# A linear-attention and MLP block on one core: the first row block of W1 loaded as two halves of its columns

## The chip, the cores and the metric

The kernel runs on one core of a Trainium2 chip. The metric is the device time of one execution in microseconds; for the kernel before it is 205.89 us, the median of three runs.

## The reference

The input x has 2048 tokens of width 640. It is normalized per token, and the result feeds two branches whose outputs are added to x. Cut to what matters:

```python
xn = layernorm(x)                         # 2048 x 640, no scale or offset
# branch A: linear attention, 32 heads of 20
q, k, v = split(xn @ wqkv)                # wqkv is 640 x 1920
phi = lambda t: where(t > 0, t + 1, exp(t)) + 1e-6
o = phi(q) @ (phi(k)^T v) / (phi(q) . sum(phi(k)) + 1e-6)
# branch B: MLP
h = gelu(xn @ w1 + b1)                    # w1 is 640 x 1536
out = x + o @ wo + (h @ w2 + b2)          # w2 is 1536 x 640
```

All tensors are bf16.

## The kernel before, in words

The kernel is written for each engine by hand. A small planner (`Pl.ins`) records every instruction on its engine in the order of the Python text, and puts a semaphore wait ahead of an instruction wherever a resource that it reads or writes was last touched by another engine or a DMA. The resources are names such as `r_W1[k]` (row block k of W1), `r_x[t]` (token tile t of x) and `r_xnT[t]` (the transposed normalized tile t); each DMA has its own semaphore. Nothing reorders the instructions afterwards, so the order in the text is the order on each engine, and an instruction that waits holds up everything behind it on its engine.

Tokens come in 16 tiles of 128. The 640 rows of W1 are five row blocks of 128 (`DT` = 5, index k), and its 1536 columns are twelve column blocks of 128 (`JT` = 12, index jb). The hidden layer is computed first, transposed: for each jb, five matmuls with the stationary block `W1[:, k, jb]` and the moving tile `xnT[:, k, tokens]` add up in PSUM, and ScalarE applies the gelu into `HG`. After that follow the keys (L563, L569), the products of phi(k) with xn (L596, L605), the queries (L648), the small matrices of the attention (L658 to L712), and the output matmuls (L768, L779), which end the kernel.

The change is in the first microseconds, where x and W1 arrive while TensorE has nothing to do yet. SyncE's queue issues the loads in this order; the second part of x tile 0 goes from ScalarE's queue at the same time:

```python
dma_x(1, 1)
dma_w1(0)
dma_w1(1)
dma_w1(2)
dma_x(2, 1)
dma_w1(3)
dma_x(3, 1)
dma_w1(4)
```

`dma_w1(k)` moves one row block of 128 rows with 1536 columns, 3072 bytes a row. Four loads of two x tiles each follow, and then DMA transposes that wait for normalized tiles.

Meanwhile TensorE runs fillers (L321) and six matmuls on constants that open banks 0 to 5 (L453). VectorE computes the statistics of tiles 0 and 1 (`ln_half` L357, `ln_aggr` L365), GpSimd the reciprocal root (L367), and VectorE the normalization (`ln_norm` L381). TensorE transposes tile 0 in three parts and tile 1 in two (`tr_part` L342); ScalarE copies them to `xnT` (`cp_part` L350), except for the second part of tile 1, which is VectorE's (L351).

The first two token tiles are then computed in an order of their own, by `hk` (L439), which does the matmuls of one jb for given row blocks k and tiles, with all twelve column blocks of two tiles held in six PSUM banks. This order lets TensorE begin with row block 0 alone:

- k=0 for tile 0, jb 0 to 11 (12 matmuls of 128 columns);
- "T1": the transposes of tile 1 (5, L342);
- k=1 for tile 0, then k=0 and k=1 for tile 1 (36 matmuls);
- k=2 for both tiles (12 matmuls of 256 columns), then k=3 for jb 0 to 7;
- "T2": the transposes of tile 2 (`transp`, 5, L389);
- k=4 for jb 0 to 7, then k=3 and k=4 for jb 8 to 11.

With the last k of an odd jb the gelus of two column blocks follow on ScalarE (L446). Tiles 2 and 3 come next in packs of four column blocks (`h_pack`, L423), and the others in units of two and four tiles (`h_unit`, L408). `h_pack` and `h_unit` read all of `r_W1`. Later in the kernel W1's memory is used again for other tensors, whose first writers list all of `r_W1` too.

Of the kernel before, what the change touches and what calls it, by code (L numbers as in the profile page):

```python
# [112 lines left out]
def bass_parallel_sum__linear_attn_block__dense_activation_gelu__prompt_kernel(  # L113
    nc: bass.Bass, A_x, A_wqkv, A_wo, B_x, B_w1, B_b1, B_w2, B_b2, out):
    Batch, S, D = A_x.shape
    F = B_w1.shape[1]
# [5 lines left out]
    DT = D // P  # L122
    JT = F // P
# [15 lines left out]
    R_ = Pl.res  # L139

    with contextlib.ExitStack() as es:
# [13 lines left out]
        W1 = W1f[:].rearrange("p (k f) -> p k f", k=DT)  # L155
# [54 lines left out]
        def bank(b, lo=0, hi=512):  # L210
            return ps[:, b * 512 + lo: b * 512 + hi]
# [6 lines left out]
        r_xb = [R_("xb%d" % t) for t in range(NT)]  # L218
        r_xn = [[R_("xn%d_%d" % (t, i)) for i in range(2 if t == 0 else 1)] for t in range(NT)]
        r_xnT = [[R_("xnT%d_%d" % (t, i)) for i in range((3, 2)[t] if t < 2 else 1)] for t in range(NT)]  # L220
        r_W1 = [R_("W1_%d" % k) for k in range(DT)]
        r_Wk = R_("Wk")
        r_Wq, r_Wv, r_W2 = R_("Wq"), R_("Wv"), R_("W2")
        r_Wo = [R_("Wo%d" % w) for w in range(NW)]
# [27 lines left out]
        w1v = B_w1.rearrange("(k p) n -> p k n", p=P)  # L252
# [7 lines left out]
        def dma(eng, dst, src, writes, reads=()):  # L260
            Pl.ins(eng, lambda e: e.dma_start(dst, src), reads=reads, writes=writes, dma=True)  # L261
# [4 lines left out]
        def dma_x(t, n):  # L266
            dma("sync", x_in[:, t:t + n, :], xv[t * P:(t + n) * P, :].rearrange("(t p) d -> p t d", p=P),
                sum(r_x[t:t + n], []))

        def dma_w1(k):  # L270
            dma("sync", W1[:, k, :], w1v[:, k, :], [r_W1[k]])

        XA = 3 * P
        for i, (lo, hi) in enumerate(((0, XA), (XA, D))):
            dma(("sync", s_)[i], x_in[:, 0, lo:hi], xv[0:P, lo:hi], [r_x[0][i]])
        dma_x(1, 1)
        dma_w1(0)
        dma_w1(1)
        dma_w1(2)
        dma_x(2, 1)  # L280
        dma_w1(3)
# [14 lines left out]
               reads=[r_ident], writes=[r_ident])  # L296
# [39 lines left out]
        def xT(t, k):  # L336
            return r_xnT[t][next(i for i, (_, lo, hi, _) in enumerate(PARTS[t]) if lo <= k < hi)]
# [97 lines left out]
        def hk(t, n, jb, ks):  # L435
            b = jb // 2
            o = (jb % 2) * 2 * P + t * P
            tok = slice(t * P, (t + n) * P)
            Pl.ins(pe, [(lambda e, k=k: e.matmul(  # L439
                bank(b, o, o + n * P), W1[:, k, jb * P:(jb + 1) * P], xnT[:, k, tok],  # L440
                start=False, stop=(jb % 2 == 1 and k == DT - 1))) for k in ks],
                reads=[r_W1[k] for k in ks] + [xT(u, k) for u in range(t, t + n) for k in ks],
                writes=[B_[b]])
            if DT - 1 in ks and jb % 2:
                for i in range(2):
                    Pl.ins(s_, lambda e, i=i, jb=jb - 1 + i: e.activation(  # L446
                        HG[:, jb, tok], bank(b, i * n * P, (i + 1) * n * P), ACT.Gelu_apprx_tanh, bias=b1c[:, jb:jb + 1]),
                        reads=[B_[b], r_b1c], writes=[r_HG[u][jb - 1 + i] for u in range(t, t + n)])
# [3 lines left out]
        for b in range(6):  # L452
            Pl.ins(pe, lambda e, b=b: e.matmul(  # L453
                bank(b), nc.const_aps.tensor(1.0, [P, P], BF16), pm[:].broadcast_to((P, 512)), start=True, stop=False),
                reads=[r_pm], writes=[B_[b]])
# [49 lines left out]
        for u in plan:  # L505
            if u == "T1":
                for i in range(2):
                    tr_part(1, i)
                    cp_part(1, i)
                ln_stats(2)  # L510
                ln_half(3, 0)
                ln_half(3, 1)
                ln_norm(2)
                ln_aggr(3)
            elif u == "T2":
                at(7)
                b = transp(2)
                ln_norm(3)
                xnT_dma(3)
                xnT_copy(2, b)  # L520
                ln_stats(4)
                ln_rest()
            elif len(u) == 2:
                h_pack(*u)
            elif len(u) == 4:
                hk(*u)
            else:
                h_unit(*u)
# [29 lines left out]
        for c in range(NC):  # L558
            ts = range(c * CH, c * CH + CH)
            cc = slice(c * CW, (c + 1) * CW)  # L560
            for t in ts:
# [4 lines left out]
                    reads=r_xnT[t] + [r_Wk], writes=[B_[b]])  # L566
# [5 lines left out]
                reads=sum((r_xnT[t] for t in ts), []) + [r_Wk], writes=[B_[b]])  # L572
            phi(bank(b), b, 1, PKT[:, cc], r_PKT[c], [])
            dma_t("sync", PK[:, c * CH:(c + 1) * CH, MW:D], PKT[:, cc], [r_PKr[c]] + sum((r_x[t] for t in ts), []),
                  reads=[r_PKT[c]])
# [12 lines left out]
        for k in range(DT):  # L588
            for i in range(DT):
                Pl.ins(g, lambda e, k=k, i=i: e.tensor_copy(plain(Wqkv[:, k, D:2 * D], i), parts(Wqkv[:, k, 0:D], i)),  # L590
                       reads=[r_Wq], writes=[r_Wk, r_WqP])
# [248 lines left out]
        t = NT - 1  # L840
        xb(t)
        tok = slice(t * P, (t + 1) * P)
        for i, (lo, hi, b) in enumerate([(0, 3 * P, bb[1]), (3 * P, MW, bb[2])]):
# [5 lines left out]
                reads=[B_[b], r_xb[t]], writes=[r_o] + ([r_out[s]] if i == 0 else []))  # L849
# [41 lines left out]
```

## Time and profile before

| | |
|---|---|
| median of 3 runs | 205.89 us (205.84 to 206.03) |
| the profiled execution | 206.18 us, span 204.5 us |
| TensorE busy | 200.7 us, 98% of the span, 1238 matmuls |
| TensorE weight loads busy | 104.6 us, 51% |
| VectorE, ScalarE, GpSimd busy | 108.8, 71.3, 33.5 us |
| DMA queue of SyncE | 17.86 MB, 33.8% of 16 engines' span |
| loads of W1, issue to landing | 4.6 us the shortest, 5.6 the median, 6.1 the longest |

The span is the part of the execution in which engines work; the time of the profiled execution is 1.7 us longer. TensorE is busy for nearly all of it. A busy share is an average over the kernel, so for a change in the first microseconds the timeline and the waits of that stretch count, and not the table. The granted TensorE clock is full in all slices. The five loads of W1's row blocks are issued from 1.73 to 4.99 us, and the DMA engines are busy from about 2 us to 13 us.

### The profile page before, as it was taken

What the parts mean: (1) busy time and instruction counts of PE and PEld (TensorE: products, weight loads), DVE (VectorE), ACT (ScalarE), POOL (GpSimd) and SP (SyncE); (2) the same over time, 40 slices, a digit from 0 to 9 for tenths busy, and PEclk for the clock granted to TensorE, in tenths of its full rate; (3) what the DMA queues carried; (4) which work ended last, traced back from release to release, by engine and by line L of the source; (5) the groups of instructions that cost most, each with busy time, mean ns of one, the idle gap of its engine ahead of it and who ended that gap; (6) DMA issues with size and microseconds to landing.
All of it is one profiled execution on the core that took longest, in us unless ns stands there. A gap on an engine that the chain in (4) does not pass through costs nothing.

```text
span 204.5 us, 3358 instructions
## 1 busy us (share of the span) xinstructions
PE 200.7 (98%) x1238; PEld 104.6 (51%) x1238; DVE 108.8 (53%) x238; ACT 71.3 (35%) x144; POOL 33.5 (16%) x84
## 2 busy tenths in 40 slices
PE   8899999999999999999999999999999999999995
PEld 3899884444444444444546444544444444444443
DVE  3588764000007889399748888834634723513131
ACT  2269995666676555121154464500000000000000
POOL 3245637300000001897000200000000000000000
PEclk9999999999999999999999999999999999999999
DMA  5997595799800111100050001239985511102301
GB/s 170 370 265 93 116 179 101 216 329 353 282 7 0 26 26 26 29 0 0 0 99 2 0 0 21 86 52 201 326 217 131 140 42 52 51 26 51 79 29 51
DMA packets 35769, 21.70 MB, mean 106 GB/s; under 512 B 22696, under 2 KB 35112, under 8 KB 35752
## 3 DMA queue, kind: packets, MB, share of 16 engines
q1 hardware_dynamic: 31696, 17.86, 33.8%
q10 hardware_dynamic: 4056, 3.61, 6.6%
q8 instruction: 10, 0.16, 0.4%
q14 instruction: 7, 0.06, 0.1%
HBM read 13.08 MB, written 2.62 MB: 77 GB/s over the span
## 4 chain that ended last, share of the span: by engine, by line
PE 96%; DMA 2%; SPq 0%; DVE 0%; issue 0%
PE ps L768 29%; PE ps L408 19%; PE ps L648 11%; PE ps L596 8%; PE ps L563 8%; PE ps L779 7%; PE ps L439 3%; PE ps L423 3%; DMA W<-in_B_w_dram 2%; PE ps L605 2%; PE ps L569 2%; PE ps L702 1%; PE ps L658 1%; PE ps L712 1%; SPq L261 0%; DVE W L847 0%
## 5 line engine op out<-in xcount | busy, mean ns | idle before, releaser
L768 PE MATMUL ps<-W,HG 128*128 128x512 bf16 (+2 forms) x204 | 43.9, 367 | 0.0
L408 PE MATMUL ps<-xnT,W 128*128 128x512 bf16 (+1 forms) x225 | 39.1, 336 | 0.0
L768 PEld LDWEIGHTS ps<-W,HG 128*128 128x128 bf16 x204 | 19.5, 98 | 22.2 <-ACT Msb L684 0.2
L551 ACT ACTIVATE ek<-ps 128x512 bf16<-128x512 f32 x40 | 23.8, 597 | 19.6 <-DVE PQ L554 9.3
L408 PEld LDWEIGHTS ps<-xnT,W 128*128 128x128 bf16 x225 | 21.9, 98 | 16.8 <-issue 0.3
L412 ACT ACTIVATE HG<-ps,b1c 128x512 bf16<-128x512 f32 (+1 forms) x45 | 26.3, 670 | 11.3 <-PE ps L408 10.8
L552 DVE TENSOR_SCALAR ek<-ek 128x512 bf16<-128x512 bf16 x40 | 11.4, 286 | 28.3 <-ACT ek L551 28.3
L792 DVE TENSOR_TENSOR W<-ps,xnT 128x512 bf16<-128x512 f32 x15 | 10.4, 691 | 24.9 <-PE ps L768 19.6
L648 PE MATMUL ps<-xnT,Wqkv 128*128 128x512 bf16 x100 | 21.9, 379 | 0.0
L768 PE MATMUL ps<-Msb,PQ 128*128 128x512 bf16 (+2 forms) x85 | 19.6, 366 | 0.0
L563 PE MATMUL ps<-Wqkv,xnT 128*128 128x512 bf16 x80 | 17.9, 379 | 0.0
L596 PE MATMUL ps<-xPK,xn_tm 128*128 128x512 bf16 x80 | 17.4, 379 | 0.0
L590 POOL COPY Wqkv<-Wqkv 128x128 bf16<-128x128 bf16 x25 | 13.5, 540 | 22.4 <-PE ps L569 20.9
L357 DVE BATCH_NORM_STATS2 stats<-xPK 128x6 f32<-128x320 bf16 (+2 forms) x32 | 13.9, 478 | 5.3 <-DMA xPK<-in_A_x_dram 5.3
L648 PEld LDWEIGHTS ps<-xnT,Wqkv 128*128 128x128 bf16 x100 | 9.6, 98 | 11.5
L554 DVE SCALAR_TENSOR_TENSOR PQ<-ps,ek 128x512 bf16<-128x512 f32 x20 | 13.8, 691 | 2.1
L768 PEld LDWEIGHTS ps<-Msb,PQ 128*128 128x128 bf16 x85 | 8.1, 98 | 9.2
L596 PEld LDWEIGHTS ps<-xPK,xn_tm 128*128 128x128 bf16 x80 | 7.8, 98 | 9.4
L563 PEld LDWEIGHTS ps<-Wqkv,xnT 128*128 128x128 bf16 x80 | 7.8, 98 | 9.4
L554 DVE SCALAR_TENSOR_TENSOR xPK<-ps,ek 128x512 bf16<-128x512 f32 x16 | 11.1, 692 | 1.7
L619 DVE TENSOR_TENSOR Msb<-Msb,xPK 128x640 f32<-128x640 f32 x14 | 11.6, 826 | 0.5
L367 POOL TENSOR_TENSOR rstd<-aggr,mhalf 128x1 f32<-128x1 f32 x16 | 10.0, 623 | 7.4 <-DVE aggr L365 7.4
(77 smaller groups left out, 156.6 us busy)
## 6 DMA issues: line engine op xcount, KB each, us to landing
Wqkv<-in_A_wqkv_dram SPq DMA_DIRECT2D x3, 800.0 KB, 6.8
xnT<-in_A_x_dram SPq DMA_DIRECT2D x4, 512.0 KB, 6.5
W<-in_B_w_dram SPq DMA_DIRECT2D x5, 384.0 KB, 5.6
W<-in_B_w_dram SPq DMA_DIRECT2D x1, 1920.0 KB, 13.4
out_dram<-W ACTq DMA_DIRECT2D x15, 128.0 KB, 1.7
xn_tm<-rden ACTq DMA_DIRECT2D x12, 128.0 KB, 3.8
xPK<-in_A_x_dram SPq DMA_DIRECT2D x4, 320.0 KB, 6.9
Wo<-in_A_wo_dram SPq DMA_DIRECT2D x8, 160.0 KB, 8.9
```

The source lines that it names most:

```text
L357: Pl.ins(v, lambda e: e.bn_stats(stats[:, s, 6 * h:6 * h + 6], x_in[:, t, lo:hi]), reads=[r_x[t][min(h, len(r_x[t]) - 1)]], writes=[r_stat ...
L408: Pl.ins(pe, [(lambda e, k=k: e.matmul(bank(b, 0, w), W1[:, k, jb * P:(jb + 1) * P], xnT[:, k, tok], start=(k == 0), stop=(k == DT - 1))) ...
L412: Pl.ins(s_, lambda e: e.activation(HG[:, jb, tok], bank(b, 0, w), ACT.Gelu_apprx_tanh, bias=b1c[:, jb:jb + 1]), reads=[B_[b], r_b1c], wri ...
L551: Pl.ins(s_, lambda e: e.activation(e2, src, ACT.Exp), reads=br, writes=[r_ek[s]])
L554: Pl.ins(v, lambda e: e.scalar_tensor_tensor(out=d2, in0=src, scalar=0.0, in1=e2, op0=ALU.max, op1=ALU.add), reads=br + [r_ek[s]], writes= ...
L563: Pl.ins(pe, [(lambda e, k=k, b=b, t=t: e.matmul(bank(b), xnT[:, k, t * P:(t + 1) * P], Wqkv[:, k, D:D + MW], start=(k == 0), stop=(k == D ...
L590: Pl.ins(g, lambda e, k=k, i=i: e.tensor_copy(plain(Wqkv[:, k, D:2 * D], i), parts(Wqkv[:, k, 0:D], i)), reads=[r_Wq], writes=[r_Wk, r_WqP])
L596: Pl.ins(pe, lambda e, t=t, b=b, f=f, i=i: e.matmul(bank(b), xn_tm[:, t, f * P:(f + 1) * P], PK[:, t, 0:MW], start=(i == 0), stop=(i == NT ...
L619: Pl.ins(v, lambda e, t=t: e.tensor_tensor(out=zsum, in0=zsum, in1=PK[:, t, :], op=ALU.add), reads=[r_PK[t], r_PKr[t // CH], r_zsum], writ ...
L648: Pl.ins(pe, [(lambda e, k=k, j=j, b=b: e.matmul(bank(b), Wqkv[:, k, D + j * P:D + (j + 1) * P], xnT[:, k, cc], start=(k == 0), stop=(k == ...
L768: Pl.ins(pe, [(lambda e, i=i, x=x, bk=bk: e.matmul(bank(bk, 0, x[1] - x[0]), seq[i][0], seq[i][1][:, x[0]:x[1]], start=(i == 0), stop=(i = ...
L779: Pl.ins(pe, lambda e, i=i: e.matmul(bank(b), seq[i][0], seq[i][1], start=(i == 0), stop=(i == NS - 1)), reads=seq[i][2], writes=[B_[b]], ...
```

## The change

Row block 0 of W1 is loaded by two DMAs, columns 0 to 767 and 768 to 1535, issued one after the other from SyncE's queue where the one DMA stood. Each has its own resource and its own semaphore; `r_W1` now has six entries. The matmuls of row block 0 wait for the half that holds their column block: jb 0 to 5 for the first, jb 6 to 11 for the second. The other row blocks are loaded as before.

```diff
-        r_W1 = [R_("W1_%d" % k) for k in range(DT)]
+        r_W1 = [R_("W1_%d" % i) for i in range(DT + 1)]
...
         def dma_w1(k):
-            dma("sync", W1[:, k, :], w1v[:, k, :], [r_W1[k]])
+            dma("sync", W1[:, k, :], w1v[:, k, :], [r_W1[k + 1]])
+
+        def rW(k, jb):
+            return r_W1[k + 1 if k or 2 * jb >= JT else 0]
...
         dma_x(1, 1)
-        dma_w1(0)
+        for i in range(2):
+            half = slice(i * F // 2, (i + 1) * F // 2)
+            dma("sync", W1[:, 0, half], w1v[:, 0, half], [r_W1[i]])
         dma_w1(1)
...
-                reads=[r_W1[k] for k in ks] + [xT(u, k) for u in range(t, t + n) for k in ks],
+                reads=[rW(k, jb) for k in ks] + [xT(u, k) for u in range(t, t + n) for k in ks],
```

On TensorE this adds one wait, at the seventh of the twelve matmuls k=0 of tile 0; on SyncE's queue it adds one issue. The order of all other instructions is unchanged, and their source lines move down by five from `hk` and the functions before it on.

## The prediction

> **What bounds the kernel now.** I read the page first, then the chain of work that ended last, then the timeline of the first 14 us.
>
> ```profile
> PE 200.7 (98%) x1238; PEld 104.6 (51%) x1238; DVE 108.8 (53%) x238; ACT 71.3 (35%) x144; POOL 33.5 (16%) x84
> ...
> PE 96%; DMA 2%; SPq 0%; DVE 0%; issue 0%
> ```
>
> TensorE carries 96% of the chain; DMA has 2%, and the chain in order of time (start, duration, what) shows that all of it is one transfer:
>
> ```profile
> 1.73 4.59 DMA W<-in_B_w_dram
> 6.32 0.05 issue
> 6.37 0.84 PE ps L439 x12
> 7.21 0.28 PE ps L342 x5
> 7.49 4.22 PE ps L439 x56
> 11.71 0.28 PE ps L389 x5
> 11.99 1.75 PE ps L439 x16
> 13.73 6.70 PE ps L423 x120
> 20.43 38.97 PE ps L408 x225
> ```
>
> The first row block of W1, issued at 1.73, lands at 6.32, and the twelve k=0 matmuls start. From there TensorE is listed without a break to 202.17. So only what moves TensorE in the first 14 us, and is not lost again before L423, moves the end; behind L423 a shift passes through one for one.
>
> The chain says nothing of the second block. In the timeline of the weight loads and of ScalarE (start, duration, engine, line):
>
> ```profile
> 5.67 0.28 ACT L350 ACTIVATE xnT<-ps 128x128 bf16<-128x128 bf16 x1 [2.92 <-PE ps L342]
> 5.79 0.23 PEld L342 LDWEIGHTS ps<-ident,xn_tm 128*128 128x128 bf16 x4 [0.23 <-DVE xn_tm L381]
> ...
> 6.36 0.67 PEld L439 LDWEIGHTS ps<-xnT,W 128*128 128x128 bf16 x12 [0.34 <-DMA W<-in_B_w_dram]
> 6.99 0.32 PEld L342 LDWEIGHTS ps<-ident,xn_tm 128*128 128x128 bf16 x5
> 7.34 4.09 PEld L439 LDWEIGHTS ps<-xnT,W 128*128 128x128 bf16 x56
> ```
>
> Five transposes start from 6.994; at the 56 ns from one load to the next that the trace's records have here, the following load would come at 7.273. The first k=1 load starts at 7.336, 63 ns late. The source view of the DMA issue at 2.2 us, W1's second block, gives why:
>
> ```profile
> L261 SPq DMA_DIRECT2D W<-in_B_w_dram x1: 432/432/432, 2.2 to 2.2; - x1
> ...
> DMA to landing us min/median/max: 5.1/5.1/5.1
> ```
>
> 2.198 plus 5.1 is 7.3; the trace's semaphore records put the last of its 16 increments at 7.295, and 7.295 + 0.041 = 7.336. The first block has the same step: last increment 6.321, load 6.363. So TensorE waits twice, for block 0 and, directly behind, for block 1. The second wait is so short that the list of waits does not show it, but it is the **gate**: whatever k=0 does, k=1 starts 0.041 us after block 1 has landed.
>
> Behind it the gates have room. Block 2 is down at 8.243 and first used at 9.36, block 3 at 9.649 and 10.67, block 4 at 11.103 and 11.82. Token tile 2's transposes (L389) load at 11.44; its normalization ends at 11.34, and a load follows such an end by 0.05 (5.35 to 5.40), so the slack is 0.05 us. That chain hangs on the load of x tile 3, landed at 10.086 behind the W1 blocks in the same queue.
>
> **What the Trainium skill says.** "DMA: Bandwidth & Descriptors", section on queues, rings and completion order: one transfer is spread over up to 16 DMA engines, each takes its descriptors in ring order, and only the full 16 increments mean landed. The trace agrees: block 0's increments come from 4.658 to 6.321, fourteen by 5.547, two at 6.160 and 6.321. Its section on latency and other measured facts says two engines of the 16 are usually slower, for a cause it calls uncertain; the trace shows two late increments on every block, but not which engines made them. "Perfetto Trace Analysis", section on the HWDGE DMA instruction: the profiled bar of an issue is not the data movement. Here the bar is 0.43 us and the landing 4.6 to 6.1 us after issue. "DMA: Bandwidth & Descriptors", section on why small descriptors are slow, gives every packet a fixed overhead; the trace agrees, and its own durations price it below.
>
> **The change part by part.**
>
> 1. *Block 0's first half lands earlier.* Same issue time, 1.73, half the bytes. Three things then hold the first k=0 load: the landing, the copy of xnT that ScalarE ends at 5.95 (plus 0.04 to 0.05 for the semaphore), and the four transposes before it in program order, whose last load is at 5.922, next slot 5.978. The earliest start is about 6.00 against 6.363: at most 0.36 us. The landing itself is not in the trace. Bounds: not before x tile 1's last increment at 3.641, not after block 0's own 6.321. On the latest engine half of the 2.68 us between these gives 4.98; if it stalls early and streams late, four packets of 121 ns fewer give 5.84. I take 5.84; either lets TensorE start at about 6.00.
>
> 2. *A second wait, at the seventh k=0 matmul* (jb=6), for the second half. Behind it in TensorE's order are five k=0 matmuls, tile 1's transposes and all of k=1; ScalarE's and VectorE's copies of tile 1 wait for those transposes. Six matmuls at 56 ns from 6.00 end at 6.34; the second half lands at about 6.321 + 0.07 (next item), so the load goes at 6.43 and k=0 issues out by 6.77. Tile 1 is normalized at 6.73, so the transposes go at about 6.78 and are out by 7.06 to 7.1.
>
> 3. *Block 1 lands later, by the split's overhead.* The queue is full: of the answer by stretches (TensorE, weight load, VectorE, ScalarE, GpSimd busy, clock, DMA share, GB/s):
>
> ```profile
> 5.00:6.00 1.00, 0.55 (x8) 0.38 (x7) 0.72 (x4) 0.33 (x2) 0.57 (x2) 1.00 0.99 387
> 6.00:7.00 1.00, 0.83 (x16) 0.66 (x14) 0.45 (x1) 0.68 (x3) 0.17 (x1) 1.00 1.00 335
> ```
>
> The DMA engines are busy 99 to 100%, so extra packet time is delay. Median packets of this queue take 36 ns at 768 B, 55 at 1280 and 121 at 3072: 0.0368 ns per byte and 8 ns fixed. Each engine gets 16 packets of 1536 B in place of 8 of 3072: 8 x 8 = 64 ns more, and one more semaphore write of 9 ns. Sum **0.07 us**. Block 1 lands at 7.37, k=1 loads at 7.41.
>
> 4. *SP issues one transfer more.* Issues here follow each other by 0.47 us, so blocks 1 and 2, x tile 2 and all behind them are issued 0.47 later. Block 1 would be issued at 2.67; the first packets of block 0 ran 1.28 after its issue (1.73 to 3.01), which gives 3.95 for block 1, while the first engine to finish block 0 did so at 4.66. The cover is 0.7 us of backlog on the first engine and over 2 us on the latest, where the gate is; without it the cost is 0.47. SP then has its transposes queued, which wait for VectorE until 12.70 (a 6.2 us wait), so the shift ends there. ScalarE's queue is untouched. I take zero.
>
> 5. *Blocks 2 to 4 and x tiles 2 and 3* shift by the same 0.07, inside slacks of 0.7 to 1.1 for the blocks. Tile 2's transposes shift with the path: 0.07 late both, slack unchanged. Zero. Any later work sees the same bytes; one semaphore more costs nothing that the trace shows.
>
> Sum on the path: item 1 gains up to 0.36 at k=0, of which nothing passes k=1, since the wait for block 1 grows from 0.06 to about 0.35; item 3 costs 0.07. Against the profiled execution (206.18, span 204.5) that is 206.25. This execution lies 0.29 above the median of the runs, 205.89, so the runs should have **205.96**.
>
> **The rivals.**
>
> *The early start counts.* Block 1 comes earlier too, because the first touch of W1 stalls less with smaller packets: of block 0's 128 packets, 26 took over 200 ns, and their excess over 121 ns is 613 ns for each engine on average. If a third went away, block 1 would gain 0.2. TensorE can win at most 7.336 less about 7.07, that is 0.27: 205.62. Against it: nothing in the trace ties the stall to packet size, and 0.27 is under what counts as faster here.
>
> *The stall is paid twice.* Block 1 has no packet over 200 ns, so the stall belongs to the first touch of W1's first rows. If it comes again with the second half, everything behind is later by up to 0.61 + 0.07 = 0.68: 206.57, **slower**. It decides from 0.34 us of repeated stall, some 55%. For it: the second half is a transfer of its own, and the gate is the latest of 16 engines. Against: same rows and neighbouring bytes, and the four later blocks paid at most 57 ns for each engine.
>
> *The issue slot is exposed*: 0.47 late, 206.36. The DMA share of 0.99 speaks against it.
>
> *The first half does not land early*, because the latest engine finishes both halves together. Then k=0 starts at 6.36 as now, and the gate still gives +0.07: the same 205.96.
>
> **How the numbers follow.** About 0.2% (0.41 us) is what a measurement of this kernel can tell from no change. Forecast, with the half that is not early: 0.60. Early start counts: 0.14, of which 0.04 for a bound that I have misread. Stall paid twice or slot exposed: 0.26, of which 0.20 beyond 0.41. So faster 0.04, same 0.76, slower 0.20. The likeliest case alone is 205.85 to 206.10. The range takes in most of the gain and half of the slower case: 205.70 to 206.45.
>
> **What would show it.** In the profile after, the first k=0 load should start near 6.0, with a short wait at the seventh; the first k=1 load should stand 0.04 behind block 1's last increment, near 7.41, after a wait of about 0.3 us on DMA; the chain should name W1's second block as its DMA. I am wrong if block 1 lands before 7.25 or after 7.6, if k=1 starts well behind its landing, or if a new gap opens at tile 2's transposes.

## The result, and the profile after

The kernel became slower: 207.05 us, median of six runs (206.62 to 207.38), against 206.00 for the kernel before in its own six (205.84 to 206.40). The ratio is 1.0046, 95% interval 1.0029 to 1.0063, so about 0.95 us were lost. Ratios are taken over all executions of both kernels and need not be those of the medians, which are 1.05 apart here. One execution of all the runs below, at 208.99 us, ran in a slower state of the chip and is in no ratio. The forecast was 205.96 and the range ended at 206.45. The profiled execution took 207.27, 1.09 more than the one shown of before.

The timeline of the weight loads of the kernel after (start, duration, line, count; lines have moved down by five):

```profile
6.08 0.69 PEld L444 LDWEIGHTS ps<-xnT,W 128*128 128x128 bf16 x12
6.79 0.35 PEld L347 LDWEIGHTS ps<-ident,xn_tm 128*128 128x128 bf16 x5
8.43 4.09 PEld L444 LDWEIGHTS ps<-xnT,W 128*128 128x128 bf16 x56 [1.28 <-DMA W<-in_B_w_dram]
12.53 0.37 PEld L394 LDWEIGHTS ps<-ident,xn_tm 128*128 128x128 bf16 x5
12.86 1.14 PEld L444 LDWEIGHTS ps<-xnT,W 128*128 128x128 bf16 x11
```

In the kernel before, tile 2's transposes (L389 there) started at 11.44:

```profile
11.44 0.38 PEld L389 LDWEIGHTS ps<-ident,xn_tm 128*128 128x128 bf16 x5
```

The split does what it says: k=0 starts at 6.08 in place of 6.36, and tile 1's transposes at 6.79 in place of 6.99. Then TensorE stands still until 8.43. In the list of waits (total, times, longest) a wait that was too short to be listed before is now one of the longest of TensorE:

```profile
PEld ps L444 <- DMA W<-in_B_w_dram: 1.3, 1, 1.3
PE ps L444 <- DMA W<-in_B_w_dram: 1.1, 1, 1.1
```

The chain of waits names the transfer, as the longest pieces in order of time show; its DMA is now W1's block 1, issued at 2.67:

```profile
2.67 5.72 DMA W<-in_B_w_dram
8.43 4.37 PE ps L444 x56
14.83 6.70 PE ps L428 x120
```

L428 starts at 14.83 in place of 13.73 (L423 then), 1.10 later, and the profiled execution is 1.09 longer. All the loss is made before that point.

Block 1's last increment comes at 8.388 in the trace's semaphore records, 7.295 before. Fifteen of its sixteen have come by 7.035, when before fifteen had come by 7.11; the longest packet of the stretch took 1.63 us. The last increment then stays 0.85 to 1.15 us behind the fifteenth on every load from block 2 to block 4. But the others are late too: the median increment (the mean of the eighth and the ninth) of block 1 is at 6.29 after and 5.99 before, that of block 4 at 10.98 and 10.27. x tile 3 lands at 11.19 in place of 10.09, its median increment comes at 9.98 in place of 9.31, and tile 2's transposes load at 12.53 in place of 11.44. So two things stand in this profile: the whole queue is late, by 0.3 to 0.7 us, and one increment of each load comes later still.

### The profile page after: what moved, and what is told of

Its sections match the earlier page's. It is cut to its first block, busy times and chain, and to the rows that moved or that the text cites. A ratio compares the mean times of both kernels' runs of the same rounds, so it can differ in the third digit from the quotient of the medians.

```text
span 205.5 us, 3336 instructions
## 1 busy us (share of the span) xinstructions
PE 199.5 (97%) x1221; PEld 104.7 (51%) x1238; DVE 108.9 (53%) x238; ACT 71.3 (35%) x144; POOL 33.4 (16%) x84
## 4 chain that ended last, share of the span: by engine, by line
PE 71%; DVE 18%; DMA 6%; issue 2%; SPq 1%; ACT 1%; DVEq 0%
PE ps L773 28%; PE ps L413 19%; PE ps L784 7%; PE ps L568 6%; DVE Msb L624 6%; DVE PQ L559 3%; PE ps L428 3%; PE ps L444 3%; DMA W<-in_B_w_dram 3%; PE ps L653 3%; DVE ek L557 2%; DVE xPK L559 2%; DMA Msb<-Msb 2%; DMA xPK<-Msb 1%; PE ps L574 1%
```

## The experiments

At first two theories competed. **P**: packets of half the size cost at the first touch of W1. **Q**: one more transfer in front of block 1 costs, through its place in the queue or the later issue of what follows. Each kernel ran beside the kernel before on its chip; "before" stands at 206.0 to 206.1 in all of them.

**The kernel after once more.**

> The kernel after, unchanged, on the chip of the other runs of this group. Both theories expect +0.6 to +1.3 us against the kernel before, the k=1 loads 0.04 us behind the landing of W1's second block, and that landing between 7.9 and 8.7 us instead of 7.3. If one DMA engine's stall in the first profile was chance, the landing is near 7.4 and the time within 0.2 us of before.

206.83 against 206.07, ratio 1.0041 (1.0026 to 1.0057). Block 1 lands at 8.16, k=1 loads at 8.20. The loss is no chance of one profile. But here too the last increments decide: fourteen of block 1's had come by 6.58 (by 6.61 in the kernel before), the last two at 7.94 and 8.16. Tile 2's transposes waited as well:

```profile
8.20 4.09 PEld L444 LDWEIGHTS ps<-xnT,W 128*128 128x128 bf16 x56 [1.08 <-DMA W<-in_B_w_dram]
12.44 0.28 PEld L394 LDWEIGHTS ps<-ident,xn_tm 128*128 128x128 bf16 x5 [0.15 <-DVE xn_tm L386]
```

**An added transfer with almost no bytes.**

```diff
         dma_w1(0)
+        dma("sync", b2t[:], B_b2[MW:D].rearrange("(p a) -> p a", a=1), [r_b2t])
         dma_w1(1)
...
-        dma("sync", b2t[:], B_b2[MW:D].rearrange("(p a) -> p a", a=1), [r_b2t])
```

> Block 0 stays one transfer; the small load of the last 128 values of b2 (2 bytes a row) moves up from far behind to the place between W1's blocks 0 and 1, so that one more transfer stands ahead of block 1 in SyncE's queue and everything behind it is issued 0.47 us later, with almost no bytes and no 1536-byte packets. Theory Q (a transfer more in the queue, and the later issue, costs): block 1 lands near 8.2, +0.6 to +1.2 us, as in the kernel after. Theory P (packets of half size at the first touch of W1 cost): block 1 lands at 7.3 to 7.45, 0 to +0.15 us.

207.04, ratio 1.0057 (1.0037 to 1.0078). Block 1 lands at 8.27. The loss is there without halves. Here block 0 was late as well, at 7.17, though it was issued at 1.73 as before, so this profile has its wait mostly ahead of k=0, and a later issue doesn't explain that part:

```profile
7.21 0.67 PEld L440 LDWEIGHTS ps<-xnT,W 128*128 128x128 bf16 x12 [0.97 <-DMA W<-in_B_w_dram]
8.31 4.09 PEld L440 LDWEIGHTS ps<-xnT,W 128*128 128x128 bf16 x56 [0.15 <-DMA W<-in_B_w_dram]
```

**Half-size packets without an added transfer.**

```diff
-        dma_w1(0)
+        dma("sync", W1[:, 0, :].rearrange("p (a f) -> p a f", a=2), w1v[:, 0:2, 0:F // 2], [r_W1[0]])
```

> Block 0 stays one transfer with one semaphore, but of 256 packets of 1536 bytes; its second half of columns is filled with block 1's first half, so the output is not the reference's. No issue is added and no other one moves. Theory P: block 1 lands near 8.2, +0.7 to +1.3 us (k=0 also starts later, at 6.4 to 7). Theory Q: block 1 lands 0.07 later, 7.4, and +0.05 to +0.15 us.

206.06 against 206.07, ratio 0.9998 (0.9985 to 1.0010). P is refuted, and with it the packet overhead as anything that can be measured here. The profile is of the longest execution of this kernel (206.89), with block 1 at 7.57.

**Two halves by rows.**

```diff
         for i in range(2):
-            half = slice(i * F // 2, (i + 1) * F // 2)
-            dma("sync", W1[:, 0, half], w1v[:, 0, half], [r_W1[i]])
+            half = slice(i * P // 2, (i + 1) * P // 2)
+            dma("sync", W1[half, 0, :], w1v[half, 0, :], [r_W1[i]])
...  # every k=0 matmul reads r_W1[0] and r_W1[1]
```

> Block 0 as two transfers of 64 rows each, packets of 3072 bytes, 4 for each DMA engine and transfer; every k=0 matmul waits for both. One issue more than before, as many packets and bytes. Theory Q: block 1 lands near 8.2, +0.6 to +1.2 us. Theory P: block 1 at 7.3 to 7.45, 0 to +0.15 us.

206.90, ratio 1.0042 (1.0029 to 1.0055): as slow as the kernel after, with packets of 3072 bytes. Its issues of 64 rows take longer: block 1 was issued at 2.97, 0.77 later than before. But it landed at 6.93, earlier than either theory said. TensorE lost its time elsewhere:

```profile
6.45 0.68 PEld L444 LDWEIGHTS ps<-xnT,W 128*128 128x128 bf16 x12
7.17 0.36 PEld L347 LDWEIGHTS ps<-ident,xn_tm 128*128 128x128 bf16 x5
7.48 4.13 PEld L444 LDWEIGHTS ps<-xnT,W 128*128 128x128 bf16 x56
12.30 0.28 PEld L394 LDWEIGHTS ps<-ident,xn_tm 128*128 128x128 bf16 x5 [0.70 <-DVE xn_tm L386]
```

k=1 was only 0.14 late, but tile 2's transposes waited 0.70 for the normalization, since x tile 3 had landed at 10.99. So there is a **second gate**, and block 1's landing by itself isn't the measure. P was gone; Q had to be divided: **I**, the later issue of block 1 and what follows, and **D**, one transfer more wherever it stands.

**Later issue, nothing added.** The activation's record is moved up so that the DMA can wait for it; ScalarE's order is unchanged.

```diff
         dma_w1(0)
-        dma_w1(1)
+        r_late = R_("late")
+        ...  # ScalarE's first activation also writes r_late
+        dma("sync", W1[:, 1, :], w1v[:, 1, :], [r_W1[1]], [r_late])
...
```

> The kernel before with nothing added to the queue, but the issue of W1's block 1 waits for ScalarE's first activation (which ends at 2.74 us), so block 1 and all behind it are issued at about 2.8 in place of 2.2. Theory I (what costs is that block 1 is issued later, so that the DMA engines come to it before it is ready): block 1 lands at 8.0 to 8.8, +0.7 to +1.4 us. Theory D (what costs is one more transfer in the queue, whenever it is issued): block 1 lands at 7.3 to 7.5, 0 to +0.2 us.

206.55 against 206.02, ratio 1.0027 (1.0017 to 1.0037). Block 1 was issued at 2.78, block 2 at 3.15, which is nearly the kernel after's timing (2.67, 3.15), with no added transfer. It costs 0.53 us: less than I said, far more than D. The profile, of an execution above the median (206.94), has block 1 itself early again (6.81, not the 8.0 to 8.8 of theory I). Block 2 and tile 2's normalization hold TensorE behind k=1 instead:

```profile
7.12 3.25 PEld L440 LDWEIGHTS ps<-xnT,W 128*128 128x128 bf16 x48
10.58 0.77 PEld L440 LDWEIGHTS ps<-xnT,W 128*128 128x128 bf16 x8 [0.21 <-DMA W<-in_B_w_dram]
12.29 0.28 PEld L392 LDWEIGHTS ps<-ident,xn_tm 128*128 128x128 bf16 x5 [0.95 <-DVE xn_tm L384]
```

**The second half from ScalarE's queue**, run twice.

```diff
-            dma("sync", W1[:, 0, half], w1v[:, 0, half], [r_W1[i]])
+            dma(("sync", s_)[i], W1[:, 0, half], w1v[:, 0, half], [r_W1[i]])
```

> The kernel after, with the second half of block 0 issued from ScalarE's queue, ahead of its table load. As many transfers as in the kernel after, but SyncE issues block 1 and all behind it at the times of the kernel before (2.2 us). Theory I: block 1 lands at 7.2 to 7.6, -0.1 to +0.2 us against before. Theory D: block 1 near 8.2, +0.6 to +1.2 us.

> The same kernel as e_half_act once more, for a profile of an execution near its median: 0 to +0.2 us, block 1 at 7.2 to 7.6, if block 1's issue time is what matters.

206.09 (ratio 1.0011, 1.0001 to 1.0021) and 206.37 (1.0019, 1.0005 to 1.0034). Most of the loss is gone although the transfers are as many as in the kernel after. Not all of it: the second interval reaches that of the kernel after, and the times that the ratios count are spread from 205.80 to 208.35. Both profiles fell on executions above the median (206.93 and 206.68), with block 1 at 8.09 and 7.99 and not at theory I's 7.2 to 7.6. In both it is the last increment that is late, 1.38 and 0.98 behind the fifteenth; the median increments, 6.00 and 5.79, are as early as before (5.99). So one late increment of sixteen can cost as much with the issue times of before; the times say that it does so less often.

**The same split at block 3.**

```diff
-        dma_w1(3)
+        for i in range(2):
+            half = slice(i * F // 2, (i + 1) * F // 2)
+            dma("sync", W1[:, 3, half], w1v[:, 3, half], [r_W1[(3, 5)[i]]])
...  # k=3 of jb 6 to 11 reads r_W1[5]
```

> The kernel before with block 3 of W1 loaded as two halves of its columns in place of block 0. As many transfers, packets and bytes as in the kernel after, but the added issue comes at about 4 us, when the DMA engines are behind with earlier transfers. Theory I: blocks 1 and 2 as before, 0 to +0.2 us. Theory D: x tile 3 and block 4 land 0.6 to 1 us later, tile 2's transposes are late, +0.5 to +0.9 us.

206.04 against 206.02, ratio 1.0004 (0.9995 to 1.0012). An added transfer costs nothing here; D is refuted. Blocks 1 and 2 keep their issue times. x tile 3 is issued 0.71 later than before (5.00 and 4.30) and lands at 9.89, not later: at this place the backlog does cover the added issue. The profile is of one of the shortest executions (205.76). It shows where the first gate would let TensorE go: block 1 at 7.00, k=1 with no wait.

```profile
6.14 0.69 PEld L441 LDWEIGHTS ps<-xnT,W 128*128 128x128 bf16 x12 [0.26 <-DMA W<-in_B_w_dram]
6.78 0.32 PEld L344 LDWEIGHTS ps<-ident,xn_tm 128*128 128x128 bf16 x5
7.06 4.13 PEld L441 LDWEIGHTS ps<-xnT,W 128*128 128x128 bf16 x56
```

**More delay, and delay from block 2 on.** Both wait for the third matmul of L453; the first holds back block 1 and all loads behind it, the second block 2 and all behind it. The records of these loads move behind that matmul in the Python text.

```diff
-                reads=[r_pm], writes=[B_[b]])
+                reads=[r_pm], writes=[B_[b]] + ([r_late] if b == 2 else []))
...
-        dma_w1(1)      # the second kernel: dma_w1(2)
+        dma("sync", W1[:, 1, :], w1v[:, 1, :], [r_W1[1]], [r_late])
...
```

> As e_delay, no transfer added, but block 1 and all behind it wait for the third of the six matmuls on constants (L453, ends near 3.4 us), so they are issued 1.2 us later than before. If the cost follows the issue time (theory I), about twice that of e_delay or more: block 1 lands at 8.4 to 9.4, +1.1 to +1.8 us. If a late issue only sets off one stall of a fixed size: +0.4 to +0.9 us.

207.58, ratio 1.0078 (1.0050 to 1.0105). Block 1 was issued at 3.59 and landed at 8.28 in the profile, which is of the shortest execution (206.98):

```profile
8.33 4.09 PEld L430 LDWEIGHTS ps<-xnT,W 128*128 128x128 bf16 x56 [1.18 <-DMA W<-in_B_w_dram]
```

By the medians 1.40 us of delay cost 1.47, where 0.58 cost 0.53: the cost grows with the delay, it is no single stall of fixed size.

> Block 1 is issued at 2.2 us as before; block 2 and all behind it wait for the same matmul and are issued near 3.4, 0.7 us later than before. If the cost arises at block 1, which the engines reach before it is ready: block 1 at 7.3, x tile 3 at 10.0 to 10.3, 0 to +0.2 us. If it is the lateness of the whole queue: x tile 3 lands 0.7 later, near 10.8, and tile 2's transposes hold TensorE, +0.5 to +0.8 us.

206.81, ratio 1.0025 (1.0014 to 1.0036). Block 1, issued at 2.20, landed at 7.28 as before; the profile is of a shorter execution than the median (206.43). Block 2, issued 0.92 later than before, and x tile 3 at 10.53 were late, and the second gate held TensorE:

```profile
7.32 4.09 PEld L431 LDWEIGHTS ps<-xnT,W 128*128 128x128 bf16 x56
11.84 0.28 PEld L381 LDWEIGHTS ps<-ident,xn_tm 128*128 128x128 bf16 x5 [0.43 <-DVE xn_tm L373]
```

So the lateness of all that follows counts, not a stall at block 1 alone.

**The first gate moved.**

```diff
-        plan = ... k_list(0, 1, [1]) + k_list(1, 1, [0]) + k_list(1, 1, [1])
+        plan = ... k_list(1, 1, [0]) + k_list(0, 1, [1]) + k_list(1, 1, [1])
```

> The kernel after, with TensorE's k=0 matmuls of tile 1 moved ahead of the k=1 matmuls of tile 0, so that block 1 is first needed 0.67 us later. If the wait for block 1 is the only gate, TensorE starts them at about 7.7 (after the copies of tile 1) and k=1 near 8.4: +0.3 to +0.5 us against before. If the late queue holds a second gate (x tile 3, then tile 2's transposes, near 12.5 instead of 11.44): +0.7 to +1.1 us, with the wait moved to L394.

206.73, ratio 1.0029 (1.0018 to 1.0041): between the two answers. In its profile block 1 had landed at 6.69 and TensorE waited 0.55 for ScalarE's copy of tile 1, with nothing at L394. It doesn't tell the gates apart; it only shows that the new order has a price of its own.

**Earlier issue**, by moving an x load to ScalarE's queue: tile 1, and then all of tile 0, the latter with the whole block 0 and with the halves.

```diff
-        dma_x(1, 1)
+        dma(s_, x_in[:, 1:2, :], xv[P:2 * P, :].rearrange("(t p) d -> p t d", p=P), r_x[1])
...
-        for i, (lo, hi) in enumerate(((0, XA), (XA, D))):
-            dma(("sync", s_)[i], x_in[:, 0, lo:hi], xv[0:P, lo:hi], [r_x[0][i]])
+        dma(s_, x_in[:, 0, :], xv[0:P, :], r_x[0])
```

> The kernel before, block 0 whole, with the load of x tile 1 issued from ScalarE's queue; as many transfers, W1's blocks and all behind them issued 0.47 us earlier. Theory I: block 1 lands at 6.4 to 7.0, k=1 starts at about 7.1 to 7.3, -0.1 to -0.3 us. Theory D: same number of transfers, no change, -0.1 to +0.1 us.

207.08, ratio 1.0067 (1.0041 to 1.0093): slower, and both answers missed. Block 0 landed at 4.89, but x tile 1, now beside W1 on the other queue, at 5.06 in place of 3.64, and VectorE takes tile 1's statistics ahead of tile 0's normalization. k=0 started at 6.89.

> The kernel before, block 0 whole, with all of x tile 0 in one load from ScalarE's queue; SyncE starts with x tile 1, so W1's blocks and all behind them are issued 0.47 us earlier than before, with one transfer less. If the time follows the issue times in this direction too: block 1 at 6.5 to 7.0, TensorE held by tile 0's later normalization and tile 1's transposes instead, -0.1 to -0.3 us, faster than both kernels. If the queue is limited by bytes once it runs at the issue times of before: -0.1 to +0.1 us. If x tiles 0 and 1 arriving together late hold VectorE: +0.2 to +0.5.

206.80, ratio 1.0054 (1.0034 to 1.0074): 0.73 slower, beyond all three answers. The queue did what theory I says: issued 0.47 earlier, block 1 landed at 6.01, 1.28 earlier than before, and x tile 3 at 8.99. TensorE doesn't wait for a DMA at all; it waits for tile 0, whose single load landed at 3.89 in place of 3.04 and 3.23:

```profile
6.25 0.10 PEld L341 LDWEIGHTS ps<-ident,xn_tm 128*128 128x128 bf16 x1 [1.56 <-DVE xn_tm L380]
...
6.92 0.69 PEld L438 LDWEIGHTS ps<-xnT,W 128*128 128x128 bf16 x12
7.63 0.36 PEld L341 LDWEIGHTS ps<-ident,xn_tm 128*128 128x128 bf16 x5
7.95 4.13 PEld L438 LDWEIGHTS ps<-xnT,W 128*128 128x128 bf16 x56
```

> The kernel after, halves of block 0 and all, with all of x tile 0 from ScalarE's queue; SyncE issues block 1 and all behind it at the times of the kernel before (2.2 us), and all of W1 stays on SyncE's queue. If the lost time of the kernel after is its later issues and nothing else: -0.2 to +0.2 us against before. If the halves cost by themselves: +0.5 to +1.0.

206.68, ratio 1.0031 (1.0020 to 1.0042): the time is tile 0's again (k=0 at 6.84, no DMA wait later), so it can't say what the halves cost. What it does show is the queue: with the issue times of before, halves and all, block 1 lands at 6.79 and x tile 3 at 10.01, not later than before.

No kernel here beats the kernel before.

**The runs side by side.** Issue and landing are read from the trace. "Stalled" is worked out from its packet records: for blocks 0 and 1 of W1, as many packets as they have in order of start, the time of every packet above the median for its size, added up and divided by 16 engines. "Median" is x tile 3's median increment. Each row is one profile.

| kernel | block 1, 2 issued | block 1 lands | x tile 3 lands | median | stalled | ratio |
|---|---|---|---|---|---|---|
| before | 2.20, 2.67 | 7.30 | 10.09 | 9.31 | 0.63 | 1 |
| half-size packets | 2.20, 2.71 | 7.57 | 10.35 | 9.11 | 0.49 | 0.9998 |
| split at block 3 | 2.20, 2.67 | 7.00 | 9.89 | 9.06 | 0.52 | 1.0004 |
| second half on the other queue | 2.20, 2.68 | 8.09 | 10.93 | 9.30 | 0.82 | 1.0011 |
| the same again | 2.20, 2.68 | 7.99 | 10.77 | 8.99 | 0.44 | 1.0019 |
| halves, tile 0 on the other queue | 2.20, 2.67 | 6.79 | 10.01 | 9.32 | 0.60 | gated by tile 0 |
| tile 0 on the other queue | 1.73, 2.20 | 6.01 | 8.99 | 8.61 | 0.11 | gated by tile 0 |
| tile 1 on the other queue | 1.73, 2.20 | 7.14 | 9.91 | 9.16 | 0.45 | gated by tile 1 |
| after | 2.67, 3.15 | 8.39 | 11.19 | 9.98 | 0.93 | 1.0046 |
| after, once more | 2.67, 3.15 | 8.16 | 11.13 | 9.85 | 0.73 | 1.0041 |
| tiny transfer added | 2.67, 3.15 | 8.27 | 11.13 | 10.92 | 1.73 | 1.0057 |
| halves by rows | 2.97, 3.60 | 6.93 | 10.99 | 9.97 | 0.77 | 1.0042 |
| other order of k | 2.67, 3.14 | 6.69 | 10.46 | 9.81 | 0.78 | 1.0029 |
| later, none added | 2.78, 3.15 | 6.81 | 10.98 | 9.60 | 1.04 | 1.0027 |
| later from block 2 | 2.20, 3.59 | 7.28 | 10.53 | 9.86 | 1.06 | 1.0025 |
| much later | 3.59, 3.97 | 8.28 | 11.09 | 10.46 | 1.13 | 1.0078 |

The landings of x tile 3 overlap: with the issue times of before, the two kernels with the second half on the other queue have 10.93 and 10.77, and with later ones the other order of k has 10.46. Its median increment doesn't: it comes by 9.32 in all eight profiles with the issue times of before or earlier, and from 9.60 on in all eight with later ones. So the issue times move the queue as a whole, and one or two late increments of the sixteen come on top of that, in either group.

## Why the prediction was wrong

**The gate was right.** k=1 loads 0.04 us behind block 1's last increment (8.388 and 8.430; 8.16 and 8.20 in the second run), k=0 started at 6.08 where I had 6.00, and nothing of it passed k=1. The first half landed at 5.11, between my two estimates, and the second at 6.04, ahead even of the first matmul, so the second wait that I priced costs nothing.

**Item 3 had the packet time right, and it didn't matter.** A packet of 1536 bytes took 65 ns, the 64.5 that my fit gives, and the run with such packets and no added transfer lost nothing, within 0.2 to 0.3 us; 0.07 is too little to be seen.

**Item 4 is the step that failed.** I gave the added issue 0.47 us of delay, held 0.7 to over 2 us of backlog against it, and took zero. That cover failed. Later issue with nothing added cost 0.53 us for 0.58 of delay and 1.47 for 1.40, so it can carry over half of the 0.95; and the same split at block 3 is free. The rival "the issue slot is exposed" named the place; its size, 0.47, was half of what was lost.

The backlog itself was there. In the kernel after, the first packet of 3072 bytes (block 1's) started at 4.11, and the first engine had done with the second half at 4.44. But the packets that came then stalled: 17 of the first 128 of 3072 bytes, block 1's but for a few, took over 200 ns, and none of block 1's did before. Fourteen of block 1's increments were hardly late (by 6.73, and by 6.61 before), the last one was, and it is the last that the gate waits for; there I had counted over 2 us of cover. With halves and the issue times of before, 12 to 17 such packets are seen too, so that part doesn't hang on the issue time alone.

One reading of item 4 is off, without weight: SyncE's queue waits from 7.99 to 12.70 for its first transpose, 4.7 us and not 6.2.

What misled me stands in item 3: I read the DMA share of 99 to 100% as a queue that is full of bytes. The same view of the kernel before, two other stretches (the last two numbers are the DMA share and GB/s):

```profile
3.00:4.00 1.00, 1.00 (x4) 0.37 (x3) 0.89 (x2) 0.00 (x0) 0.23 (x1) 1.00 1.08 220
11.00:12.00 1.00, 1.00 (x14) 0.93 (x12) 0.46 (x2) 0.00 (x0) 0.45 (x1) 1.00 1.07 383
```

The share is the same and the bytes differ by 1.7. A packet that stalls counts as busy: in the first stretch one of 3072 bytes, from 3.95 on, took 1132 ns, where the median is 121. And the kernel after moves less from 4 to 6 us: 252 and 323 GB/s, against 320 and 387. The first line is of the kernel before, the other two of the kernel after:

```profile
4.00:5.00 1.00, 1.00 (x8) 0.48 (x6) 0.94 (x3) 0.00 (x0) 0.65 (x2) 1.00 0.89 320
4.00:5.00 1.00, 0.65 (x8) 0.36 (x5) 0.92 (x3) 0.00 (x0) 0.63 (x2) 1.00 1.10 252
5.00:6.00 1.00, 0.53 (x7) 0.36 (x7) 0.74 (x4) 0.32 (x2) 0.57 (x2) 1.00 0.94 323
```

I had the stalls in hand, 0.61 us for each engine, and treated them as a fixed price of the first touch. The table shows them larger where the issue is late: 0.73 to 1.73, against 0.11 to 0.63 with the issue times of before or earlier, with one exception at 0.82. Counted over all packets that start from 2 to 10 us it is 1.30 to 1.80 us for each engine against 0.64 to 1.22. That is one profile for each row, and goes with the issue times; that the late issue makes the stalls isn't shown. The rival "the stall is paid twice" had more stall too, but tied it to the second half; it comes without halves.

**Item 5 failed with item 4.** Tile 2's transposes are late by as much as k=1 in the kernel after (1.09 both), so they did not hold TensorE there, as I said; in its second run they waited 0.15. But that is not because they move with TensorE: x tile 3 itself lands 1.10 later. Where block 1 came early, that second gate held TensorE by itself (0.70 and 0.95 in the halves by rows and the delay without a transfer).

**What stays open.** Delay alone cost 0.53 (ratio interval 1.0017 to 1.0037), the kernels with an added transfer in that place 0.76 to 1.05 (the second run of the kernel after: 1.0026 to 1.0057). The intervals overlap; whether the added transfer has a price of its own besides the delay isn't settled. The second half on the other queue, with the issue times of before, left a loss of 0.07 and 0.26 by the medians. No run restored the issue times on one queue without making tile 0 late. Nor do the runs say what a stalled packet waits for, or which engine is hit.

## What to carry to other kernels

In the first microseconds of this kernel the time of issue of the loads moved the landing of the data, even where the DMA share read 100%: look at the GB/s beside the share before an added issue is called hidden. Cutting the first load so that work can begin sooner moves every load behind it, so price the next loads that are waited for, one by one, with the issue slot added. If a load is to be cut, cut one behind the loads that gate the start: at block 3, issued at about 4 us, it was free. And a landing is the last of sixteen increments: look at the others too before one profile's landing is taken for the queue's.

## What had not been expected of the hardware

One increment of sixteen can hold a transfer for over a microsecond, and the lateness stays: block 1 of the kernel after had fifteen increments by 7.04 and the last at 8.39, and x tile 3, four loads on, still had fifteen by 10.34 and the last at 11.19. Which load is hit first changes from profile to profile (block 1 there, block 2 in the delay without a transfer, x tile 1 in the halves by rows). Putting a load on a second queue frees the first one's slot, but the load itself came later: x tile 1, issued at the same time, landed 1.42 us later beside W1 (5.06 and 3.64), and x tile 0 as one larger load 0.66 us later than its later part had (3.89 and 3.23).
